# Retention of the last seven token groups: 128-token chunks on half arrays, or 64-token chunks on quarters

## The chip, the cores and the metric

The kernel is one program on one core of a Trainium2 chip. The core has a matrix engine (TensorE, PE in the profile, with its weight loads on a line of their own, PEld), a vector engine (VectorE, DVE), a scalar engine (ScalarE, ACT), a general engine (GpSimd, POOL) and a queue that issues DMA transfers (SyncE, SP). Matrix products land in PSUM, eight banks of 128 partitions by 512 floats. The metric is the device time of one launch in microseconds (us), the median over runs. Everything is computed in float32 precision or better.

## The reference

Three stages, each feeding the next: retention attention (4 batches, 8 heads, 576 tokens, 64 dimensions a head), a SoLU layer with layer norm between two weight matrices, and four ReLU experts that are summed with the weights of the tokens.

```python
# retention: q, k, v are [4, 8, 576, 64]
scores = (1 / sqrt(64)) * q @ k.T
gamma = 1 - 2 ** (-5 - arange(8))                  # one decay a head
Dmat = where(rel >= 0, gamma ** rel, 0)            # rel = query position - key position
x = (scores * Dmat) @ v                            # -> [2304 tokens, 512]
# SoLU
h = x @ w_in                                       # 512 -> 1024
solu = h * softmax(h)
ln = (solu - mean) / sqrt(var + 1e-6) * g_ln
x = ln @ w_out                                     # 1024 -> 512
# experts
p = domain_probs / sum(domain_probs)
out = sum(p[:, e] * (relu(x @ w1[e]) @ w2[e]) for e in range(4))
```

The decay lets retention be written in chunks: inside a chunk of tokens the scores are formed and masked ("qk", the DVE product "ret", and "pv"), and all that lies before the chunk enters through one 64x64 state a head ("cross"), to which each chunk adds its own keys times values ("st").

## The kernel before

The 2304 tokens are 18 groups of 128 (`NG`). Nine groups are two batches, since a batch is 4.5 groups; the fifth group of such a period (`g % 9 == 4`) therefore ends one batch in its first 64 tokens and begins the next in its last 64. The layers run in three passes of six groups (`NPASS`, `GP`). A token group of SoLU is: `h_mm` (24 products of 128x512, in two halves of 12, into a tile of the pool psA), maximum and exponential (`chain1`, `chain1e`), the softmax product with its sum (`chain2`), a squared sum on ACT (`chain2s`), the layer norm's factors on POOL (`chain3a`, `chain3m`) and its application on ACT (`chain3b`, an Identity activation on `acc`), eight transposes on PE (`tr`) whose result is split into a high and a low part by ACT (`t_hi`, two copies to `h`) and DVE (`t_lo`, two differences). After a pass's six groups `x2_mm` multiplies by w_out (24 products `b<-h,wB` a step), and the experts follow.

Retention of groups 0 to 10 is part of an order written out by hand (`ORDER`), at the start of the program. That of groups 11 to 17 (`OWN`) is not: from the first experts on, a `Recorder` collects the operations of a stretch (all of these carry line 149 in the profile, 150 in the changed kernel), gives each a due time from the costs of the PE work in program order, and lists them by a simulated schedule (`flush`): on each engine the operation with the earliest due time that is ready in the simulation goes next, on PE at most 150 operations ahead of program order, and preferably one of the group marked last (`mark`). The engines then run the lists in order; a wait at the head of a list holds all behind it. The first two groups' work (11 and 12) is recorded at the end of the experts of pass 0, the rest in pass 1's loop, between the `h_mm` halves of groups 6 to 11.

One group g of `OWN` consists of
- `att_load`, `att_v`, `att_q`: 1 MB of q, k (both layouts) and v into `tmp` (odd g) or the region `dec` (even g), and POOL's products with decays;
- `att_st`: 8 products k.T v, `sbank<-tmp 128x64` or `sbank<-dec`, which add to the state in the PSUM bank `sbank`. Two of them stand side by side on the array (column halves);
- `att_qk`: 8 products `64x128` into two banks b, two side by side on row halves;
- `att_ret`: DVE multiplies the two banks by the decay mask, 128x512 each;
- `att_state`: ACT copies the state from `sbank` into one of two buffers `states`, two copies of 64x256;
- `att_pv`: 8 products ret times v into one bank b, and 8 products state times q ("cross", `b<-tmp,st`), both on column halves, 128 columns at a time;
- `att_xh`, `att_xl`: the result's high part (ACT, 128x512) and low part (DVE).

The float32 products of retention count as two records each in the profile (x16 for 8 products). The three banks b are handed out in turn (`next_b`), also to the transposes of `tr`.

```python
for i in range(GP):                      # pass 1, groups 6 to 11
    g = g0 + i
    h_mm(g, 0)
    if own and i < 5:
        att_last(OWN[i + 1]); att_store(OWN[i + 1])
        if i + 3 < len(OWN): att_pre(OWN[i + 3])
        att_first(OWN[i + 2])
    h_mm(g, 1)
    if own and i == 4: att_last(OWN[6]); att_store(OWN[6])
```

Of the kernel before, what the change touches and what calls it, by code (L numbers as in the profile page):

```python
# [2 lines left out]

# [7 lines left out]
F32 = mybir.dt.float32  # L11
# [21 lines left out]
NJ = 9  # L33
# [59 lines left out]
class Recorder:  # L93
# [67 lines left out]
    def flush(self, done=True):  # L161
# [27 lines left out]
        waiting, order = [], []  # L189
        pe = [op for op in ops if op.engine == "PE"]  # L190
        at, idle, now = 0, 0.0, self.now
        for op in ops:
            if not left[op]:
                heapq.heappush(waiting, (ready_at[op], op.index, op))
        while len(order) < len(ops):
# [5 lines left out]
            for e in FIXED:  # L201
                if free[e] > late or not queue[e] or (e == "SP" and self.dma > late + DEPTH):
                    continue
                can = [r for r in queue[e] if not (r[2].port and self.port > late)]
                can = [r for r in can if all(busy.get(b, 0) <= late for b in r[2].banks)]
                if e == "PE":
                    while at < len(pe) and pe[at].start is not None:
                        at += 1
                    can = [r for r in can if r[2].index <= pe[at].index + AHEAD]
                    can = [r for r in can if r[2].group == self.last] or can  # L210
                if not can:
                    continue
                best = min(can)
                queue[e].remove(best)
                op = best[2]
                moved = True
                if e == "PE":
                    self.last = op.group
                    idle += now - max(free[e], begin)
                if e == "SP":  # L220
                    free[e] = now + ISSUE
                    self.dma = max(self.dma, now) + op.cost - FIXED[e]
                    op.end = self.dma + FIXED[e]
                else:
                    op.end = free[e] = now + op.cost
                if op.port:
                    self.port = op.end
                for b in op.banks:
                    busy[b] = op.end if e == "PE" else op.end + LATENCY
                op.start = now  # L230
                order.append(op)
                for s in op.after:
                    left[s] -= 1
                    ready_at[s] = max(ready_at[s], op.end + (0 if s.engine == e != "SP" else LATENCY))
                    if not left[s]:
                        heapq.heappush(waiting, (ready_at[s], s.index, s))
# [28 lines left out]
def retention_solu_moe(  # L265
# [80 lines left out]
    tmp = big.tile([P, 4608], F32, name="tmp")  # L346
    hx = big.tile([P, 3 * BLK], F32R, name="hx")
    pb = big.tile([P, 2 * BLK], F32, name="pb")
    hT = [None, None]
    area = {}  # L350

# [175 lines left out]
    def att_v(g, eng=nc.gpsimd):  # L527
        j = g % NJ
        t = grp(g)
        if j < NJ - 1:  # L530
            v, vd = (t[:, i : i + 512].rearrange("p (h t) -> p h t", h=H) for i in (1536, 2048))
            eng.tensor_tensor(
                out=vd, in0=v, in1=vtab[:, j].unsqueeze(2).to_broadcast([P, H, 64]), op=ALU.mult
            )
# [307 lines left out]
            nc.sync.dma_start(out=dst, in_=w2b[e, m].rearrange("a p t -> p a t"))  # L842

    def probs_t():
        x = pb[:, 0 : NG * E].rearrange("p (j e) -> p j e", e=E)
        y = pb[:, 128 : 128 + NG * E].rearrange("p (e j) -> p e j", e=E)
        r = pb[:, 256 : 256 + NG]
        nc.sync.dma_start(out=x, in_=probs2)
        nc.vector.tensor_reduce(out=r, in_=x, axis=AX.X, op=ALU.add)
        nc.vector.tensor_scalar_add(out=r, in0=r, scalar1=1e-9)  # L850
# [429 lines left out]
    def att_pre(g):  # L1280
        att_load(g)
        att_v(g)
        att_q(g)

    def att_first(g):
        att_st(g)
        att_qk(g)
        att_ret(g)
        att_state(g)

    def att_last(g):
        att_pv(g)
        att_xh(g)
        att_xl(g)

    def w_in_load(i):
        nc.sync.dma_start(out=wA[:, 2048 * i : 2048 * i + 2048].bitcast(F32), in_=s_in[i])
# [219 lines left out]
```

## Time and profile before

| | us |
|---|---|
| median of 3 runs (lowest, highest) | 1029.25 (1028.58, 1031.97) |
| the profiled execution | 1028.85 |
| its span in the trace | 1027.1 |
| PE busy | 1006.8 (98%) |
| DVE, ACT, POOL busy | 616.2, 526.4, 448.4 |

The chain of waits (the work that ended last, followed back) runs over PE for 93% of the span, and PE's granted clock is full in all forty slices of the page. So a stretch is read on PE: a group of PE work begins where the one before has ended unless the timeline shows an idle time in brackets. The retention that is changed lies between 382.60 us (the first st of group 11) and about 443 us; the stretch up to 389.20, before the first psA, holds no other PE work and is called the head below. The layer-norm chain and transposes of groups 8 to 11 end the stretch, and x2_mm follows.

In a timeline, the first column is the start, the second the time from the first start to the last end of the group. Ends of PE records overlap with what follows, so the time that a block takes is read from its start to the next block's start.

### The profile page before, as it was taken

What the parts mean: (1) busy time and instruction counts of PE and PEld (TensorE: products, weight loads), DVE (VectorE), ACT (ScalarE), POOL (GpSimd) and SP (SyncE); (2) the same over time, 40 slices, a digit from 0 to 9 for tenths busy, and PEclk for the clock granted to TensorE, in tenths of its full rate; (3) what the DMA queues carried; (4) which work ended last, traced back from release to release, by engine and by line L of the source; (5) the groups of instructions that cost most, each with busy time, mean ns of one, the idle gap of its engine ahead of it and who ended that gap; (6) DMA issues with size and microseconds to landing.
All of it is one profiled execution on the core that took longest, in us unless ns stands there. A gap on an engine that the chain in (4) does not pass through costs nothing.

```text
span 1027.1 us, 17077 instructions
## 1 busy us (share of the span) xinstructions
PE 1006.8 (98%) x6188; PEld 949.4 (92%) x6188; DVE 616.2 (60%) x1038; ACT 526.4 (51%) x1032; POOL 448.4 (44%) x433
## 2 busy tenths in 40 slices
PE   5999999999999999999999999999999999999998
PEld 4788998898989988899999999999899999999998
DVE  5999685586766514543736555565454736566564
ACT  3668664252534303554746556462573646555562
POOL 3443254334435012303465656564140565655554
PEclk9999999999999999999999999999999999999999
DMA  9857699899886948570847566586541748576524
GB/s 346 326 207 265 214 311 293 298 284 316 294 262 200 335 187 298 205 261 22 250 135 246 165 214 200 175 281 227 231 154 35 243 135 255 160 221 194 183 73 131
DMA packets 122788, 226.79 MB, mean 221 GB/s; under 512 B 9936, under 2 KB 57040, under 8 KB 116560
## 3 DMA queue, kind: packets, MB, share of 16 engines
q1 hardware_dynamic: 122704, 225.70, 65.9%
q8 instruction: 49, 0.80, 0.3%
q14 instruction: 35, 0.29, 0.1%
HBM read 169.00 MB, written 62.95 MB: 226 GB/s over the span
## 4 chain that ended last, share of the span: by engine, by line
PE 93%; DVE 4%; DMA 2%; ACT 1%; SPq 0%; issue 0%; ACTq 0%
PE psX L149 44%; PE b L149 29%; PE sbank L149 8%; PE psA L149 6%; DMA dec<-in_w_in 1%; DMA sx<-wA 1%; PE b L382 1%; PE b L384 1%; PE b L383 1%; PE b L604 1%; DVE wA L387 1%; PE psA L383 1%; PE psA L382 1%; PE b L610 1%; PE psA L384 0%; PE b L557 0%
## 5 line engine op out<-in xcount | busy, mean ns | idle before, releaser
L149 POOL TENSOR_TENSOR h<-tmp,h 128x384 fp32r<-128x384 f32 x128 | 129.3, 1017 | 95.0 <-ACT h L149 79.1
L149 PE MATMUL psX<-xb,wA 128*128 128x384 f32 x738 | 143.7, 334 | 0.0
L149 PEld LDWEIGHTS psX<-xb,wA 128*128 128x128 f32 x738 | 129.4, 188 | 0.3
L149 POOL TENSOR_TENSOR wA<-wA 128x512 fp32r<-128x512 f32 x74 | 97.7, 1329 | 69.6 <-ACT wA L149 69.4
L149 PE MATMUL b<-xa,wA 128*128 128x384 f32 x564 | 111.0, 334 | 0.0
L149 PEld LDWEIGHTS b<-xa,wA 128*128 128x128 f32 x564 | 99.0, 188 | 0.1
L149 ACT ACTIVATE h<-tmp 128x384 fp32r<-128x384 f32 x144 | 73.4, 521 | 30.0 <-DVE tmp L149 30.0
L149 ACT ACTIVATE tmp<-psX 128x384 f32<-128x384 f32 x122 | 59.5, 489 | 53.0 <-PE psX L149 51.1
L149 POOL TENSOR_TENSOR tmp<-tmp 128x256 f32<-128x256 f32 (+1 forms) x68 | 56.9, 853 | 57.1 <-DMA tmp<-in_w 38.3
L149 PE MATMUL psX<-wB,h 128*128 128x512 f32 x336 | 78.9, 390 | 0.0
L149 PE MATMUL psX<-xa,wA 128*128 128x384 f32 x396 | 77.4, 334 | 0.0
L149 PE MATMUL psX<-h,wA 128*128 128x384 f32 x408 | 74.9, 334 | 0.0
L149 ACT ACTIVATE tmp<-b 128x384 f32<-128x384 f32 x108 | 53.1, 492 | 42.5 <-DVE b L149 18.4
L149 PEld LDWEIGHTS psX<-wB,h 128*128 128x128 f32 x336 | 63.0, 188 | 12.8
L149 ACT ACTIVATE wA<-wA 128x512 fp32r<-128x512 f32 x74 | 46.3, 631 | 51.4 <-DMA wA<-sw 43.7
L149 PE MATMUL psA<-wA,xa 128*128 128x512 f32 x288 | 70.5, 398 | 0.8 <-DVE tmp L149 0.6
L149 PEld LDWEIGHTS psX<-h,wA 128*128 128x128 f32 x408 | 71.1, 188 | 0.0
L149 PEld LDWEIGHTS psX<-xa,wA 128*128 128x128 f32 x396 | 69.5, 188 | 0.2
L149 DVE TENSOR_TENSOR sbank<-sbank,tmp 128x384 f32<-128x384 f32 x48 | 27.2, 567 | 65.4 <-PE sbank L149 52.0
L149 PEld LDWEIGHTS psA<-wA,xa 128*128 128x128 f32 x288 | 52.7, 188 | 14.0 <-DVE tmp L149 1.0
L149 POOL TENSOR_TENSOR wC<-wC 128x512 fp32r<-128x512 f32 x38 | 50.7, 1342 | 29.0 <-ACT wC L149 28.9
L149 DVE SCALAR_TENSOR_TENSOR tmp<-b,tmp 128x384 f32<-128x384 f32 x96 | 51.5, 555 | 18.6 <-ACT tmp L149 8.4
(250 smaller groups left out, 2083.0 us busy)
## 6 DMA issues: line engine op xcount, KB each, us to landing
wA<-sw SPq DMA_DIRECT2D x298, 256.0 KB, 3.1
sw<-wA SPq DMA_DIRECT2D x32, 896.0 KB, 6.6
tmp<-in_w SPq DMA_DIRECT2D x24, 512.0 KB, 5.5
grps<-in_qkv SPq DMA_DIRECT2D x10, 1024.0 KB, 6.3
wC<-sw SPq DMA_DIRECT2D x38, 256.0 KB, 2.8
sw<-wCf SPq DMA_DIRECT2D x32, 256.0 KB, 4.1
wA<-sin SPq DMA_DIRECT2D x8, 1024.0 KB, 6.8
wB<-sout SPq DMA_DIRECT2D x8, 1024.0 KB, 8.7
```

Source lines behind the costliest of these rows:

```text
L149: op = Op(engine, lambda: call(*args, **kw), FIXED[engine] + rate * n, port)
L382: nc.tensor.matmul(ps, lh, rh, start=first, stop=False, skip_group_check=more)
L383: nc.tensor.matmul(ps, lh, rl, start=False, stop=False, skip_group_check=more)
L384: nc.tensor.matmul(ps, ll, rh, start=False, stop=last, skip_group_check=more)
L387: (eng or nc.vector).tensor_tensor(out=dst, in0=src, in1=hi.bitcast(F32), op=ALU.subtract)
L604: nc.tensor.matmul(o[r, n], v[:, 2 * n + a], ret[:, a, n], start=n == 0, stop=j == 0 and n == NP - 1)
L610: nc.tensor.matmul(o[r, n, 0:cross], st[:, n, r], qd[:, n, 0:cross], start=False, stop=n == NP - 1)
```

## The change

- Groups 11 to 17 are cut in two chunks of 64 tokens each (`sub_chunk` numbers the nine chunks of a batch). All products inside a chunk are 64x64 and stand on a quarter of the array: qk 16 products of 64 columns for two diagonal blocks of the scores (before: 8 of 128 columns, whose lower left block was needed and upper right block masked), pv 16 products, st 8 products for each chunk, of which each uses one row half.
- The state is copied out after each chunk's st (before: once a group), into a rotation of three buffers, the third in `pb`. The last chunk of a batch forms no state. Cross is done for each chunk that is not a batch's first, from that chunk's own state.
- pv and cross of a group go to two banks b, one for each chunk, 256 columns each (before: one bank). The copies `xh` and `xl` are two of 128x256 each, ret four of 64x256; the memset for group 13 is dropped.
- The scheduler's choice on PE may take from each marked group only the first operation in program order that is not yet listed (`heads`). This rule holds for all recorded work, the transposes and x2_mm too.
- `att_v` runs for group 17 too, the first memset on POOL covers the third buffer, and `probs_t` uses a place in `pb` behind it.

```diff
--- before.py
+++ after.py
@@ -1,4 +1,5 @@
 import heapq
+from collections import deque
 from contextlib import ExitStack
 
 import numpy as np
@@ -189,6 +190,9 @@
         waiting, order = [], []
         pe = [op for op in ops if op.engine == "PE"]
         at, idle, now = 0, 0.0, self.now
+        heads = {}
+        for op in pe:
+            heads.setdefault(op.group, deque()).append(op)
         for op in ops:
             if not left[op]:
                 heapq.heappush(waiting, (ready_at[op], op.index, op))
@@ -207,6 +211,7 @@
                     while at < len(pe) and pe[at].start is not None:
                         at += 1
                     can = [r for r in can if r[2].index <= pe[at].index + AHEAD]
+                    can = [r for r in can if r[2] is heads[r[2].group][0]]
                     can = [r for r in can if r[2].group == self.last] or can
                 if not can:
                     continue
@@ -216,6 +221,7 @@
                 moved = True
                 if e == "PE":
                     self.last = op.group
+                    heads[op.group].popleft()
                     idle += now - max(free[e], begin)
                 if e == "SP":
                     free[e] = now + ISSUE
@@ -346,6 +352,7 @@
     tmp = big.tile([P, 4608], F32, name="tmp")
     hx = big.tile([P, 3 * BLK], F32R, name="hx")
     pb = big.tile([P, 2 * BLK], F32, name="pb")
+    states.append(pb[:, 0:512].rearrange("p (n t) -> p n t", n=NP))
     hT = [None, None]
     area = {}
 
@@ -527,7 +534,7 @@
     def att_v(g, eng=nc.gpsimd):
         j = g % NJ
         t = grp(g)
-        if j < NJ - 1:
+        if j < NJ - 1 or g >= EARLY:
             v, vd = (t[:, i : i + 512].rearrange("p (h t) -> p h t", h=H) for i in (1536, 2048))
             eng.tensor_tensor(
                 out=vd, in0=v, in1=vtab[:, j].unsqueeze(2).to_broadcast([P, H, 64]), op=ALU.mult
@@ -842,9 +849,9 @@
             nc.sync.dma_start(out=dst, in_=w2b[e, m].rearrange("a p t -> p a t"))
 
     def probs_t():
-        x = pb[:, 0 : NG * E].rearrange("p (j e) -> p j e", e=E)
-        y = pb[:, 128 : 128 + NG * E].rearrange("p (e j) -> p e j", e=E)
-        r = pb[:, 256 : 256 + NG]
+        x = pb[:, 512 : 512 + NG * E].rearrange("p (j e) -> p j e", e=E)
+        y = pb[:, 600 : 600 + NG * E].rearrange("p (e j) -> p e j", e=E)
+        r = pb[:, 700 : 700 + NG]
         nc.sync.dma_start(out=x, in_=probs2)
         nc.vector.tensor_reduce(out=r, in_=x, axis=AX.X, op=ALU.add)
         nc.vector.tensor_scalar_add(out=r, in0=r, scalar1=1e-9)
@@ -1282,16 +1289,74 @@
         att_v(g)
         att_q(g)
 
+    HALVES = [slice(0, 64), slice(64, 128)]
+
+    def sub_chunk(g, s):
+        return (2 * (g % NJ) + s) % NJ
+
+    def short_state(g, s):
+        return states[(2 * g + s - 2 * EARLY + 1) % 3]
+
+    def short_st(g, s):
+        nc.mark()
+        t = grp(g)
+        kn, vd = (t[:, i : i + 512].rearrange("p (h t) -> p h t", h=H) for i in (1024, 2048))
+        q = sub_chunk(g, s)
+        if q == NJ - 1:
+            return
+        for h in range(H):
+            n, a = divmod(h, 2)
+            nc.tensor.matmul(
+                st_ps[HALVES[a], n], kn[HALVES[s], h], vd[HALVES[s], h], start=q == 0 and n == 0,
+                stop=n == NP - 1, skip_group_check=q > 0,
+            )
+        for r in HALVES:
+            copy(short_state(g, s + 1)[r, :, r], st_ps[r])
+
     def att_first(g):
-        att_st(g)
-        att_qk(g)
-        att_ret(g)
-        att_state(g)
+        short_st(g, 0)
+        nc.mark()
+        t = grp(g)
+        qt, kt = (t[:, i : i + 512].rearrange("p (n t) -> p n t", n=NP) for i in (0, 512))
+        qk = [next_b()[:, 0:256].rearrange("p (n t) -> p n t", n=NP) for a in range(2)]
+        for n in range(NP):
+            for c in HALVES:
+                for a, r in enumerate(HALVES):
+                    nc.tensor.matmul(qk[a][c, n], kt[r, n, c], qt[r, n, c], start=True, stop=True)
+        ret = (area["dec"], tmp)[g % 2][:, 3072:3584].rearrange("p (a n t) -> p a n t", a=2, n=NP)
+        for a in range(2):
+            for c in HALVES:
+                nc.vector.tensor_tensor(out=ret[c, a], in0=qk[a][c], in1=dmask[c, a, :, c], op=ALU.mult)
+        att[g] = ret
+        short_st(g, 1)
 
     def att_last(g):
-        att_pv(g)
-        att_xh(g)
-        att_xl(g)
+        nc.mark()
+        t = grp(g)
+        v = t[:, 1536:2048].rearrange("p (h t) -> p h t", h=H)
+        qd = t[:, 2560:3072].rearrange("p (n t) -> p n t", n=NP)
+        ret = att.pop(g)
+        o = [next_b()[:, 0:256].rearrange("p (n t) -> p n t", n=NP) for _ in range(2)]
+        alone = [sub_chunk(g, s) == 0 for s in range(2)]
+        for n in range(NP):
+            for s, c in enumerate(HALVES):
+                for a, r in enumerate(HALVES):
+                    nc.tensor.matmul(
+                        o[s][r, n], v[c, 2 * n + a], ret[c, a, n], start=n == 0, stop=alone[s] and n == NP - 1
+                    )
+        for s, c in enumerate(HALVES):
+            if not alone[s]:
+                for n in range(NP):
+                    for r in HALVES:
+                        nc.tensor.matmul(
+                            o[s][r, n], short_state(g, s)[:, n, r], qd[:, n, c], start=False, stop=n == NP - 1
+                        )
+        hi, lo = (att_to(g)[:, i].rearrange("p (n s t) -> s p n t", n=NP, s=2) for i in range(2))
+        for s in range(2):
+            nc.scalar.activation(out=hi[s], in_=o[s], func=AF.Copy, scale=F64_SCALE)
+            nc.vector.scalar_tensor_tensor(
+                out=lo[s], in0=o[s], scalar=F64_SCALE, in1=hi[s].bitcast(F32), op0=ALU.mult, op1=ALU.subtract
+            )
 
     def w_in_load(i):
         nc.sync.dma_start(out=wA[:, 2048 * i : 2048 * i + 2048].bitcast(F32), in_=s_in[i])
```

Recorded order on PE, the head, before: `sbank` is the state's bank, `tmp` holds group 11 and `dec` group 12, b1 is pv's bank, b2 and b0 are qk's.

```order
L149 MATMUL sbank_69<-dec_3018 64x64 x8
L149 MATMUL b1_67<-tmp_88 64x128 x4
L149 MATMUL b2_68<-dec_3018 128x128 x2
L149 MATMUL b0_66<-dec_3018 128x128 x2
L149 MATMUL b1_67<-tmp_88 64x128 x3
L149 MATMUL b1_67<-tmp_88,st1_83 64x128
L149 MATMUL b1_67<-tmp_88 64x128
L149 MATMUL b1_67<-tmp_88,st1_83 64x128 x7
L149 MATMUL psA1_1_3244<-wA_84,xa_86 128x512 x12
```

The same place after, from group 11's second st to the first psA (of qk for group 12, b0 and b1 by turns, two of fifteen rows are shown).

```order
L150 MATMUL sbank_69<-tmp_88 64x64 x8
L150 MATMUL b1_67<-tmp_88 64x64
L150 MATMUL sbank_69<-dec_3019 64x64 x8
L150 MATMUL b1_67<-tmp_88 64x64
L150 MATMUL b2_68<-tmp_88 64x64 x2
L150 MATMUL b1_67<-tmp_88,st1_83 64x64 x8
L150 MATMUL b2_68<-tmp_88,pb_90 64x64 x8
L150 MATMUL b0_66<-dec_3019 64x64
L150 MATMUL sbank_69<-dec_3019 64x64 x8
L150 MATMUL b1_67<-dec_3019 64x64
L150 MATMUL b0_66<-dec_3019 64x64
L150 MATMUL psA1_1_3303<-wA_84,xa_86 128x512 x12
```

There are now four blocks on `sbank` before the first psA instead of two, and between the second and the third stands only a single pv product.

PE at the end of the stretch, before: the last psA (`h_mm` of group 11), then the transposes `b<-tabs,acc` of groups 9 and 10 and the steps of x2_mm, `b<-h1,wB`.

```order
L149 MATMUL psA1_0_3243<-wA_84,xa_86 128x512 x12
L149 MATMUL b2_68<-tabs_75,acc_87 128x128 x4
L149 MATMUL b0_66<-tabs_75,acc_87 128x128 x4
L149 MATMUL b1_67<-h1_554,wB_85 128x384 x24
L149 MATMUL b2_68<-tabs_75,acc_87 128x128 x4
L149 MATMUL sbank_69<-tabs_75,acc_87 128x128 x4
L149 MATMUL b0_66<-h1_554,wB_85 128x384 x24
```

The same place after; the rows of `tmp` are the ends of cross of group 17.

```order
L150 MATMUL psA1_0_3302<-wA_84,xa_86 128x512 x12
L150 MATMUL b2_68<-tmp_88,st1_83 64x64 x8
L150 MATMUL b0_66<-tmp_88,pb_90 64x64 x8
L150 MATMUL b1_67<-tabs_75,acc_87 128x128 x4
L150 MATMUL b2_68<-tabs_75,acc_87 128x128 x4
L150 MATMUL b0_66<-tabs_75,acc_87 128x128 x4
L150 MATMUL b1_67<-tabs_75,acc_87 128x128 x4
L150 MATMUL b2_68<-tabs_75,acc_87 128x128 x4
L150 MATMUL sbank_69<-tabs_75,acc_87 128x128 x4
L150 MATMUL b0_66<-h1_555,wB_85 128x384 x24
L150 MATMUL b1_67<-h1_555,wB_85 128x384 x24
```

The last psA has moved ahead of pv, cross and the transposes of group 8, and the transposes of group 10 (the rows on b2 and sbank) ahead of the first step of x2_mm.

ACT's list there, after: the two `wA<-b` are xh of group 17, `h1<-b` are t_hi of group 8, `acc<-psA` is the exponential of group 11, `h2<-b` are t_hi of group 9, and `acc<-acc` is the Identity of group 10 that its transposes read.

```order
L150 ACTIVATE wA_84<-b2_68 128x4x64
L150 ACTIVATE wA_84<-b0_66 128x4x64
L150 ACTIVATE h1_555<-b1_67 128x4x128
L150 ACTIVATE h1_555<-b2_68 128x4x128
L150 ACTIVATE acc_87,stats_80<-psA1_0_3302,stats_80 128x1024
L150 ACTIVATE h2_984<-b0_66 128x4x128
L150 ACTIVATE h2_984<-b1_67 128x4x128
L150 ACTIVATE acc_87<-acc_87,stats_80 128x1024
```

Before, ACT's list held xh of group 17 and t_hi of group 8 ahead of the last psA's exponential too, but these came while PE was still at that psA.

## Rows read from the trace of the kernel before

**Rows 1.** The page: span, PE's busy time, the chain by engine.
```profile
span 1027.1 us, 17077 instructions
PE 1006.8 (98%) x6188; PEld 949.4 (92%) x6188; DVE 616.2 (60%) x1038; ACT 526.4 (51%) x1032; POOL 448.4 (44%) x433
PE 93%; DVE 4%; DMA 2%; ACT 1%; SPq 0%; issue 0%; ACTq 0%
```

**Rows 2.** Windows: stretch, busy time of each engine, granted clock, DMA share.
```profile
382.60:389.20 6.60, 6.49 (x97) 5.70 (x96) 3.33 (x5) 1.07 (x3) 0.00 (x0) 1.00 0.11 42
389.20:446.76 57.56, 57.56 (x506) 46.52 (x506) 29.30 (x49) 27.30 (x47) 15.41 (x24) 1.00 0.66 243
```

**Rows 3.** Timeline of PE: one group with narrow cross, the next whole.
```profile
402.75 0.69 PE L149 MATMUL b<-tmp,st 128*64 128x64 f32 x16
403.37 3.03 PE L149 MATMUL psA<-wA,xa 128*128 128x512 f32 x12
406.33 0.73 PE L149 MATMUL sbank<-dec 128*64 128x64 f32 x16
406.99 1.16 PE L149 MATMUL b<-dec 64*128 64x128 f32 x16
408.08 3.06 PE L149 MATMUL psA<-wA,xa 128*128 128x512 f32 x12
411.07 1.15 PE L149 MATMUL b<-dec 128*64 128x128 f32 x16
411.99 1.09 PE L149 MATMUL b<-dec,st 128*64 128x128 f32 x16
413.02 3.02 PE L149 MATMUL psA<-wA,xa 128*128 128x512 f32 x12
```

**Rows 4.** Timeline of PE: the head, in which group 11's pv starts alone.
```profile
382.60 0.73 PE L149 MATMUL sbank<-tmp 128*64 128x64 f32 x16
383.26 1.16 PE L149 MATMUL b<-tmp 64*128 64x128 f32 x16
384.35 0.73 PE L149 MATMUL sbank<-dec 128*64 128x64 f32 x16
385.20 1.09 PE L149 MATMUL b<-tmp 128*64 128x128 f32 x8
386.21 1.17 PE L149 MATMUL b<-dec 64*128 64x128 f32 x16
387.31 0.54 PE L149 MATMUL b<-tmp 128*64 128x128 f32 x3
...
389.20 3.06 PE L149 MATMUL psA<-wA,xa 128*128 128x512 f32 x12
```

**Rows 5.** Timeline of ACT and of DVE: state copies and ret in the head.
```profile
383.37 0.78 ACT L149 ACTIVATE st<-sbank 64x256 f32<-64x256 f32 x2 [31.49 <-PE sbank L149]
384.45 1.29 DVE L149 TENSOR_TENSOR tmp<-b,tabs 128x512 f32<-128x512 f32 x2 [0.99 <-PE b L149]
```

**Rows 6.** Timeline of PE: the end of the stretch.
```profile
443.07 1.09 PE L149 MATMUL b<-tabs,acc 128*128 128x128 f32 x8
443.92 3.00 PE L149 MATMUL psA<-wA,xa 128*128 128x512 f32 x12
446.76 1.03 PE L149 MATMUL b<-tabs,acc 128*128 128x128 f32 x8
447.55 4.43 PE L149 MATMUL b<-h,wB 128*128 128x384 f32 x24
451.88 0.63 PE L149 MATMUL b<-tabs,acc 128*128 128x128 f32 x4
```

**Rows 7.** Timeline of ACT: the end of the stretch.
```profile
443.17 0.60 ACT L149 ACTIVATE wA<-b 128x512 fp32r<-128x512 f32 x1 [0.53 <-PE b L149]
443.76 1.09 ACT L149 ACTIVATE h<-b 128x512 fp32r<-128x512 f32 x2
448.22 1.12 ACT L149 ACTIVATE acc<-psA,stats 128x1024 f32<-128x1024 f32 x1 [3.37 <-DVE stats L149]
449.32 1.08 ACT L149 ACTIVATE h<-b 128x512 fp32r<-128x512 f32 x2
450.28 1.25 ACT L149 ACTIVATE acc<-acc,stats 128x1024 f32<-128x1024 f32 x1
```

**Rows 8.** Timeline of DVE: the low parts of a transposed group.
```profile
444.41 1.28 DVE L149 TENSOR_TENSOR h<-b,h 128x512 fp32r<-128x512 f32 x2
```

**Rows 9.** Groups of PE instructions by form: the transposes, with idle time before them.
```profile
L149 PE MATMUL b<-tabs,acc 128*128 128x128 f32 x88 | 11.9, 274 | 0.5 <-DVE h L149 0.5
```

## Prediction

> **What bounds the kernel now.** I read the page first: PE is busy for 1006.8 of a span of 1027.1 us, and the chain that ended last runs over PE for 93% [rows 1]. Then the windows of the stretch that is changed. From the first psA at 389.20 to the end of the last at 446.76 PE is busy in all of its 57.56 us, at the full granted clock, while DVE has 29.30 and ACT 27.30 us of work; in the head before it PE is busy for 6.49 of 6.60 us, and ACT has only 1.07 us of work [rows 2]. So a microsecond more or less on PE here is a microsecond of the kernel, and work that is added to ACT, DVE or POOL is free until PE has to wait for it. The timelines say what a block of PE work takes and what stands between an engine's result and PE's next block [rows 3 to 8].
>
> **What a block costs.** I take start-to-start times. Cross on 128 columns takes 413.02 - 411.99 = 1.03 us, on 64 columns 403.37 - 402.75 = 0.62, both with a change of the array's tile shape behind them; so 64 columns fewer are worth 0.41. pv, with none behind it (cross has its shape), takes 411.99 - 411.07 = 0.92. A change of shape hence costs 1.03 - 0.92 = 0.11; by the st block (0.66 against 0.92 - 0.41 = 0.51) it is 0.15, by qk (1.09 against 0.92) 0.17 [rows 3]; by psA with and without one, 2.99 against 2.84 [rows 3, 6], 0.15. I take 0.14. A wide block is 0.92, a narrow one 0.51, and in each two tiles work side by side with eight records each.
>
> After the change all blocks are narrow. A qk or pv block has 32 records of 64 columns on four quarters, so eight a quarter: 0.51 if all four work side by side. No row shows four; if only two do, it is 16 steps, 1.02 at most (twice 0.51) and 0.92 at least (as many columns as a wide block has). I take 0.51, because the four quarters differ in rows and columns just as the pairs do that already run side by side, and keep both ends. st and cross of a chunk have 16 records on two tiles: 0.51.
>
> **The sum of blocks behind the head.** Before: 4 st, 1 narrow cross, and 16 wide blocks (5 qk, 6 pv, 5 cross): 5 x 0.51 + 16 x 0.92 = 17.3 us. After: 8 st, 5 qk, 6 pv, 11 cross, that is 30 x 0.51 = 15.3. That is 2.0 less, though products are more: the wide blocks' gain is half eaten by the doubled st and cross. Changes of shape, counted in the recorded order from the first psA to the last transposes: 26 before, 35 after, since pv and cross no longer share a shape and since single products of qk or pv have been pulled ahead of a psA four times. 9 x 0.14 = +1.3. Net -0.7.
>
> **The head.** Before, it takes 6.60 us, of which 385.20 to 386.21 is half of pv alone on one column half [rows 4]. Without waits the new one would be 9 narrow blocks (4 st, 2 qk, 1 pv, 2 cross) and 4 changes, 5.2 us, 1.4 less. But four st blocks now share the one bank `sbank`, and each waits until ACT has copied the last state out. Copies start 0.77 after an st block starts and take 0.78 for the pair [rows 4, 5]; PE goes on about 0.10 after a result (the first ret product ends at 384.45 + 0.65, pv starts at 385.20). So st follows st by 1.65 at the earliest: 382.60, 384.25, 385.90. Between the first two PE has qk, 0.51; between the second and third a single pv product. Then pv and the first chunk's cross to 386.41 + 2 x 0.51 + 0.14 = 387.57; in ACT's list the first xh stands between the two copies of the third state, so copies end at about 388.45 and the fourth st starts at 388.55, followed by the rest of qk: first psA at 388.55 + 0.51 + 0.51 + 0.14 = 389.7, against 389.20: **+0.5**. The ends are -1.4 (waits all covered) and +1.0 (quarters two at a time).
>
> **The middle.** A second st stands behind a psA in all groups from 14 to 16, so its wait (1.65 from st to st) is covered by 2.99 us of psA [rows 3]. One place is not covered: qk of group 17 needs the bank b0 of the transposes of group 7, whose second half now stands behind a psA, with pv, cross and st between, some 2.6 us of PE work, while the bank is released by a copy to h and a difference (0.54 and 0.64, half of [rows 7, 8]), possibly behind an Identity of 1.25. That is 0 to 0.7; I take **+0.4**.
>
> **The end of the stretch.** Before, the last psA ends at 446.76, and the Identity of group 10 ends at 450.28 + 1.25 = 451.53, that is 4.0 us after the transposes of group 9 have ended (447.55). PE doesn't notice: it has a step of x2_mm there, 4.33 us, and starts group 10's transposes at 451.88 [rows 6, 7]. After the change these transposes stand ahead of x2_mm, and PE's list is strict in order as far as waits go. Counting from the end of the last psA: pv and two cross blocks with two changes 1.8, transposes of groups 8 and 9, 0.85 and 0.79, then group 10 would start at 3.45. ACT meanwhile has to do, in its order: xh of chunk 2 after cross has ended, to 2.3; t_hi of group 8 from 2.45, 1.09, to 3.54; the exponential of group 11 with its read, 1.10 from start to start, to 4.64; t_hi of group 9, 1.09, to 5.73 (its second half waits for b1, which t_lo of group 8 has left by 3.7); Identity, 1.25, to 6.98. PE starts group 10's transposes at 7.08 instead of 3.45: **+3.6**. x2_mm, which could have run, is queued behind. Before, the exponential found ACT idle for 3.37 us [rows 7]: xh and t_hi of group 8 had been done during the psA. That cover is gone because the last psA has moved ahead of them. The ends: 0, if ACT were early by as much, and 3.9. Nothing is late next: x2_mm's first step started without a wait at 447.55, 0.8 us after the last psA, and would start 7 us later behind it.
>
> **The rest.** The rule `heads` also reorders the transposes beside x2_mm of pass 2. In the trace all 88 transposes together waited for 0.5 us [rows 9]; I take +0.3, between 0 and 0.7 (as large a wait again as at the bank above). Twelve further state copies of 0.39 on ACT, seven more pieces each of xh and of xl, one more product on POOL for group 17: hidden by ACT's and DVE's 30 us and POOL's 42 us without work in the stretch [rows 2], but for the waits above; without that cover the copies alone would cost 12 x 0.39 = 4.7. The larger memset lies before PE's first work, behind the first loads. The load of group 13 is issued after cross of group 11 as before, and qk's first product waits for it one psA earlier; I take 0, at most one psA of 2.99 were it late.
>
> **Sum.** 0.5 - 0.7 + 0.4 + 3.6 + 0.3 = +4.1. The profiled execution took 1028.85 us, 0.4 less than the median of 1029.25, so 1028.85 + 4.1 = 1033.0.
>
> **Rivals.**
> A. The forecast, 1033.0; its own range is 1030.5 to 1035.5.
> B. Quarters don't work four at a time. Then 11 blocks behind the head cost 0.41 to 0.51 more each, 4.5 to 5.6, and the head about 0.4 (its qk lies beside the state copies): 1033.0 + 5.4, about 1038.4. For it: no row shows more than two tiles at once, and in the st block 16 records in 0.51 us are one every 32 ns. Against it: nothing in the pairs shows a limit of records rather than of columns.
> The Trainium skill ("TensorE: Matmul & The Clock Gate", section "Wait — 56ns, not 53.3ns?") says that one matmul starts at least about 25 ns after another however small it is. By that rule the 32 records of a qk or pv block would take 0.80 us, an estimate, and 13 such blocks would make the time about 1036. The st block's 32 ns neither contradicts it nor bears it out, and I count it with B.
> C. No change: st uses one row half only, so qk's records on the other half may run beside it, as cross of another chain ran beside pv's second half in the head (three pv records from 387.31, then cross in between). Where st and qk now adjoin without a wait, about 9 times, half a block of 0.26 to 0.31 is saved: -2.6, so 1030.4.
> D. Faster: the end stall doesn't arise. Its place is the wait of group 10's transposes for the Identity; its price is 3.6; it decides if ACT reaches the Identity before PE has ended group 9's transposes. Then 1029.4 is left, and with C's overlap, which needs the same free-running PE, 1026.8; with the head's waits covered as well (-1.9) 1025. Against it: before, even with its work done ahead, ACT ended the Identity 4.77 after the last psA [rows 6, 7], and PE now has 3.45 us of work to there.
>
> **Chances.** A 0.52, B 0.20, C 0.18, D 0.10. A change under 0.3%, 3.1 us, can't be told from none here. Of A about a third lies within that bound (below 1032.3), of C nearly all, of D four tenths: within 0.36. Slower: two thirds of A and B, 0.55. Faster: 0.09. The range is 1027.0 to 1038.8: below it lies most of D, above it half of B's upper part, together under 0.2.
>
> **What would show it.** Right: three waits of PE on ACT before `sbank` blocks in the head and a first psA about 0.5 us later; qk blocks of 32 records in 0.5 to 0.7 us; one PE idle of 3 to 4 us before the third pair of transposes, put down to ACT. Wrong: qk blocks near 1 us (B); st records among qk's (C); transposes of group 10 without a wait (D); or the larger loss in a stretch that has no retention in it, which no term here has.

## The result and the profile after

The changed kernel takes 1036.35 us, the median of 9 runs (1030.81 to 1038.68), against 1029.25 before (9 runs, 1028.58 to 1031.97); the ratio is 1.0058, 95% interval 1.0038 to 1.0078, so some 6 us slower (the two medians differ by 7.1). Run again on another chip (below) it was 1.0041 [1.0025, 1.0057]. The profiled execution of it took 1034.64 us. The forecast of 1033.0 had the side and the mechanism; what it lacked is in TensorE's clock and in a gain of the list rule `heads`.

The page of the kernel after: span, busy time, chain by engine, to be laid beside [rows 1].

```profile
span 1032.8 us, 17958 instructions
PE 1006.7 (97%) x6604; PEld 948.9 (92%) x6604; DVE 618.9 (60%) x1058; ACT 530.6 (51%) x1051; POOL 444.4 (43%) x435
PE 90%; DVE 5%; DMA 2%; ACT 1%; issue 1%; POOL 0%; SPq 0%; ACTq 0%; DVEq 0%
```

PE has 416 more instructions and the same busy time, while the span is 5.7 us longer: PE is idle for longer, and in part it is busy at half its clock. To see where, I measured four stretches from the starts of the same blocks in every trace (us):

| kernel | first st starts at | head, to the first psA | middle and end, to group 11's transposes | from there to the end |
|---|---|---|---|---|
| before | 382.60 | 6.60 | 76.07 | 561.8 |
| after | 383.43 | 8.34 | 79.03 | 562.0 |
| after, run again (e5) | 383.81 | 7.08 | 79.52 | 562.0 |

The start of the first st varies from 382.60 to 387.47 over the traces, whatever the kernel, so I leave it out of all that follows. In nine of the thirteen traces, of both kinds of kernel, the granted clock is half for some 3 us or twice that near 20 us or between 46 and 53 (in after it is 0.72 from 20 to 26), long before the retention that was changed; the three latest starts (e1, e4, e9) are those of the traces whose only early fall begins near 49.

Windows of the kernel after, head and middle, with columns as in [rows 2]:

```profile
383.43:391.77 8.34, 6.87 (x193) 6.20 (x193) 3.11 (x7) 2.93 (x9) 0.00 (x0) 0.80 0.35 111
391.77:445.14 53.37, 53.37 (x761) 42.61 (x760) 29.34 (x63) 28.59 (x56) 16.35 (x25) 1.00 0.64 240
```

From the first psA to the end of the last one, PE is still busy in all of its time and at the full clock. The losses lie on either side: in the head, where 1.47 us are idle and the clock was 0.80, and behind the last psA.

Timeline of PE after: one whole group of the middle, to be laid beside [rows 3].

```profile
399.62 0.69 PE L150 MATMUL b<-tmp 64*64 64x64 f32 x30
400.13 0.64 PE L150 MATMUL sbank<-tmp 64*64 64x64 f32 x16
400.70 3.02 PE L150 MATMUL psA<-wA,xa 128*128 128x512 f32 x12
403.65 0.69 PE L150 MATMUL b<-tmp 64*64 64x64 f32 x32
404.28 0.69 PE L150 MATMUL b<-tmp,pb 128*64 128x64 f32 x16
404.89 3.04 PE L150 MATMUL psA<-wA,xa 128*128 128x512 f32 x12
```

From start to start, qk takes 0.51 us, st 0.57, pv 0.63 and cross 0.61, the last three with a change of shape behind them. (Two of this qk's 32 records stand ahead of the psA before it, from 396.42, and take 0.25 there.) The four quarters do work side by side: 30 records in 0.51 us, one every 17 ns, as many columns a quarter as a tile of a pair had in [rows 3]. By the rule of the Trainium skill that the prediction cited ("TensorE: Matmul & The Clock Gate", section "Wait — 56ns, not 53.3ns?"), 32 records would take at least about 0.80 us, an estimate; this case's trace contradicts it for records on four tiles: pv has 32 in 0.63, the change of shape included.

Timeline of PE after, the head: compare [rows 4]. In brackets is PE's idle time before the row, and what ended it.

```profile
383.43 0.62 PE L150 MATMUL sbank<-tmp 64*64 64x64 f32 x13
...
384.99 0.51 PE L150 MATMUL sbank<-tmp 64*64 64x64 f32 x10 [0.41 <-ACT pb L150]
...
386.54 1.01 PE L150 MATMUL sbank<-dec 64*64 64x64 f32 x14 [0.87 <-ACT st L150]
...
388.44 1.12 PE L150 MATMUL b<-tmp,st 128*64 128x64 f32 x16
389.35 0.90 PE L150 MATMUL b<-tmp,pb 128*64 128x64 f32 x16
...
390.69 0.62 PE L150 MATMUL sbank<-dec 64*64 64x64 f32 x14 [0.19 <-ACT st L150]
```

Three of the four st blocks wait for ACT's copy of the state before, as forecast. ACT's timeline there, beside [rows 5]:

```profile
384.15 0.78 ACT L150 ACTIVATE pb<-sbank 64x256 f32<-64x256 f32 x2 [31.45 <-PE sbank L150]
385.72 0.77 ACT L150 ACTIVATE st<-sbank 64x256 f32<-64x256 f32 x2 [0.78 <-PE sbank L150]
```

Copies start 1.57 apart (1.65 forecast). But the first cross block takes 388.44 to 389.35, 0.91 where in the middle it takes 0.51 to 0.61. That is the clock. Windows of the kernel after in the head and behind the last psA; the granted clock is the third column from the end:

```profile
386.00:387.00 1.00, 0.46 (x8) 0.47 (x10) 0.18 (x1) 0.47 (x2) 0.00 (x0) 0.75 0.00 0
387.00:389.00 2.00, 2.00 (x54) 1.88 (x52) 0.00 (x0) 0.00 (x0) 0.00 (x0) 0.50 0.03 8
452.00:454.00 2.00, 2.00 (x10) 2.00 (x11) 0.97 (x3) 1.66 (x4) 0.80 (x3) 0.50 1.02 361
455.00:460.00 5.00, 5.00 (x31) 5.00 (x30) 0.74 (x2) 1.46 (x3) 0.00 (x0) 1.00 1.05 397
```

Twice in these stretches the granted clock is half for a few us, 1.2 of 2.4 GHz, each time with or right behind PE's waits. In the kernel before it is 1.00 in the head and from 446.76 to 456.00.

Timeline of PE after, behind the last psA, beside [rows 6]:

```profile
445.07 0.69 PE L150 MATMUL b<-tmp 64*64 64x64 f32 x32
...
446.77 1.67 PE L150 MATMUL b<-tabs,acc 128*128 128x128 f32 x12
448.84 0.66 PE L150 MATMUL b<-tabs,acc 128*128 128x128 f32 x4 [0.40 <-DVE h L150]
451.86 1.12 PE L150 MATMUL b<-tabs,acc 128*128 128x128 f32 x4 [2.36 <-ACT acc L150]
452.76 1.06 PE L150 MATMUL sbank<-tabs,acc 128*128 128x128 f32 x4
```

And ACT there, beside [rows 7]:

```profile
446.42 0.85 ACT L150 ACTIVATE wA<-b 128x256 fp32r<-128x256 f32 x2 [4.74 <-PE b L150]
447.47 1.14 ACT L150 ACTIVATE h<-b 128x512 fp32r<-128x512 f32 x2 [0.19 <-PE b L150]
448.50 1.11 ACT L150 ACTIVATE acc<-psA,stats 128x1024 f32<-128x1024 f32 x1
449.59 1.08 ACT L150 ACTIVATE h<-b 128x512 fp32r<-128x512 f32 x2
450.55 1.26 ACT L150 ACTIVATE acc<-acc,stats 128x1024 f32<-128x1024 f32 x1
```

This is the chain the prediction wrote down, piece by piece: xh, t_hi of group 8, exponential, t_hi of group 9, Identity, and group 10's transposes at its end, 6.79 us behind the last psA (7.08 forecast). PE has nothing for 2.36 us, while x2_mm's first step stands behind. The transposes' group of the page's kind, beside [rows 9], has its idle time up from 0.5 to 3.3:

```profile
L150 PE MATMUL b<-tabs,acc 128*128 128x128 f32 x88 | 12.8, 284 | 3.3 <-ACT acc L150 2.4 <-DVE h L150 0.9
```

### The profile page after: what moved, and what is told of

The parts are those of the page before. It is cut to its first block, busy times and chain, and to the rows that moved or that the text cites. A ratio compares the mean times of both kernels' runs of the same rounds, so it can differ in the third digit from the quotient of the medians.

```text
span 1032.8 us, 17958 instructions
## 1 busy us (share of the span) xinstructions
PE 1006.7 (97%) x6604; PEld 948.9 (92%) x6604; DVE 618.9 (60%) x1058; ACT 530.6 (51%) x1051; POOL 444.4 (43%) x435
## 4 chain that ended last, share of the span: by engine, by line
PE 90%; DVE 5%; DMA 2%; ACT 1%; issue 1%; POOL 0%; SPq 0%; ACTq 0%; DVEq 0%
PE psX L150 43%; PE b L150 28%; PE sbank L150 8%; PE psA L150 6%; DMA sx<-wA 1%; DMA tabs<-in_tab 1%; DVE wA L394 1%; PE b L611 1%; PE b L389 1%; PE b L391 1%; PE b L390 1%; PE b L564 1%; PE psA L390 1%; PE psA L389 1%; DVE wCf L150 1%
```

## The experiments

Each time is a median over one job's runs, and each ratio is to the kernel before on the same chip. "Stretch" is head, middle and end together in the profile (before 82.67, after 87.37 and, run again, 86.60). The edits are shown in short: lines that only carry an edit through are left out.

**e1, the list rule alone**, added to the kernel before, and once more as e10.

```diff
+ heads.setdefault(op.group, []).append(op)
+ can = [r for r in can if r[2] is heads[r[2].group][0]]
+ heads[op.group].pop(0)
```

> The kernel before with nothing but the rule that PE's products of a marked group are listed in program order (heads). In its recorded order x2_mm's first step still stands between the transposes of groups 9 and 10. Theory 1 (the loss comes from the narrow chunks' places in the order, not from this rule): 1029.3 +- 1.0 us, no idle of PE over 0.5 us between 383 and 470 us, granted clock as before (0.999). Theory 2 (the rule itself costs, by stopping products that could run early): 1031 or more.

1029.63 (1027.53 to 1032.56), ratio 0.9982 [0.9967, 0.9996]. The rule costs nothing; it gains a little, and it doesn't put group 10's transposes ahead of x2_mm. The stretch is 81.51, 1.16 shorter: 0.47 in the head (6.13) and 0.67 behind it (75.40). Rows of PE in the same kernel run again (e10), head and middle:

```profile
385.68 0.43 PE L149 MATMUL b<-tmp 128*64 128x128 f32 x2 [0.16 <-DVE tmp L149]
386.04 1.39 PE L149 MATMUL b<-dec 64*128 64x128 f32 x16
387.36 0.98 PE L149 MATMUL b<-tmp 128*64 128x128 f32 x13
...
411.76 1.04 PE L149 MATMUL b<-dec,st 128*64 128x128 f32 x16
```

In the head two of pv's records stand alone ahead of qk, where before eight did [rows 4]: 0.36 for 1.01, with 1.32 for 1.10 in the qk behind them. The rest of pv and cross takes 1.89 in both, by turns before, one after the other here. In the middle cross takes 0.97 (psA starts at 412.73) for 1.03 before and st 0.61 for 0.66: the change of shape behind them costs less.

**e2, x2_mm's first step first**: the kernel after, with group 10's transposes recorded as part of the same marked piece, behind x2_mm's first step.

```diff
+ if m == 0 and p == 1: tr(g0 + GP - 2, False)   # behind x2_mm(0, 0)
- if m in (1, 2):
+ if m == 2 or (m == 1 and p > 1):
```

> The changed kernel with the transposes of group 10 listed behind the first step of x2_mm; all else as in the changed kernel. Theory 1 (the end stall is an order's doing, and the half clock behind it follows from PE's idle time): the idle of 2.4 us and the half clock from 451.5 to 454.5 go, some 3.5 us less than the changed kernel; the half clock in the head stays. Theory 2 (the clock falls for another reason): only the idle goes, 2.4 us less, and x2_mm's first products still take twice as long.

1031.95, ratio 1.0006 [0.9993, 1.0019]. PE's timeline in e2, behind cross of group 17:

```profile
450.27 0.66 PE L150 MATMUL b<-tabs,acc 128*128 128x128 f32 x4 [0.40 <-DVE h L150]
450.68 4.41 PE L150 MATMUL sbank<-h,wB 128*128 128x384 f32 x24
454.93 4.32 PE L150 MATMUL b<-h,wB 128*128 128x384 f32 x24
```

x2_mm starts without a wait, so its inputs were there; only the order kept it back. Middle and end fall from 79.03 to 75.11: the order of this one piece costs 3.9, half clock included.

**e3, the second half of each state copy of groups 11 and 12 on DVE**, and **e4, both edits**.

```diff
+ if i and g < EARLY + 2: nc.vector.tensor_copy(out=short_state(g, s + 1)[r, :, r], in_=st_ps[r])
+ else: copy(short_state(g, s + 1)[r, :, r], st_ps[r])
```

> The changed kernel with the second of the two state copies of groups 11 and 12 on DVE, so that ACT and DVE copy side by side; in the recorded order group 11's pv and cross now stand between its second st and group 12's first. Theory 1: the head (first st to first psA) falls from 8.3 us to about 6.2, of which 1.1 is the half clock that no longer comes, and the end stall stays. Theory 2 (half clock is the narrow products' doing, not the waits'): waits shrink by about 1 us, pv and cross still take 1.0 and 0.9 us instead of 0.5 each, head about 7.3.

> Both edits at once: state copies of groups 11 and 12 on ACT and DVE, and x2_mm's first step ahead of the transposes of group 10. Theory 1 (two waits and the half clock behind each are the whole loss): the changed kernel's middle, 1.7 us shorter than before, remains, so 1026.5 to 1028.5, granted clock 0.999, and a spread over runs of 3 us or less as in the kernel before. Theory 2 (half clock or spread come from the narrow products): clock 0.995 or lower in part of the runs, 1029 to 1034.

e3: 1033.97, 1.0034 [1.0020, 1.0048], with a head of 7.11; e4: 1031.42, 1.0011 [0.9998, 1.0023], head 8.57. Neither the head of 6.2 nor the 1026.5 to 1028.5 of the expectations came. Two rows of e3's DVE say why the head isn't shorter than e5's 7.08:

```profile
383.94 0.43 DVE L150 COPY pb<-sbank 64x256 f32<-64x256 f32 x1 [0.28 <-ACT pb L150]
384.40 1.55 DVE L150 TENSOR_TENSOR tmp<-b,tabs 64x256 f32<-64x256 f32 x4
```

ret now starts behind the copy, and pv waits for ret: one wait replaced another. And e4 runs the same list in the head as e3 but takes 1.46 us longer, with waits of 0.47 ahead of its second and its fourth st; its granted clock there:

```profile
390.00:394.00 4.00, 3.98 (x82) 3.61 (x85) 1.23 (x4) 0.77 (x2) 0.00 (x0) 0.57 0.38 78
```

In e3's head it was 1.00. So the fall belongs to the execution, not to the list, and costs about 1.5.

**e5, the kernel after unchanged**, and **e6, its waits filled**: three products of 256 columns between group 11's qk and its second st, six behind that st, twenty ahead of group 10's transposes. They write banks that are overwritten before they are read, and the scheduler is told that they cost next to nothing.

```diff
+ def fill(ps): nc.tensor.matmul(ps, neg[:, 0], neg.rearrange("p i t -> p (i t)"), start=True, stop=True); nc.ops[-1].cost = 1e-4
+ for _ in range(3 if (g, s) == (11, 1) else 0): fill(pool["a"][1][:, 0:256])   # before the st block
+ for _ in range(6 if (g, s) == (11, 1) else 0): fill(pool["a"][1][:, 0:256])   # behind it
+ for _ in range(20 if g == 10 else 0): fill(tps[g][1].rearrange("p n t -> p (n t)")[:, 0:256])
```

> The changed kernel unaltered, beside the next three on one chip. Theory 1: from the head's first st on it is again 4 to 6 us longer than the kernel before, with waits of 0.4 and 0.9 us in the head and 2.4 us at the end, and half clock behind at least one of them.

> The changed kernel with products into unused PSUM in the waits: 3 of 128x256 ahead of group 11's second st, 6 behind it, 20 ahead of group 10's transposes (some 0.11 us each; they compute nothing that is used). The order of all else is kept. Theory 1 (PE's idle time lets the granted clock fall): the waits stay or are filled, the clock stays at full, head about 7.2 to 7.6 instead of 8.3, x2_mm's first products at full speed, 1.5 to 2 us less than the changed kernel. Theory 2 (the narrow products by themselves, or something off PE, let it fall): half clock as before in the head, no gain.

e5: 1035.76 (1033.0 to 1037.85), 1.0041 [1.0025, 1.0057]; the mean granted clock over its runs is 0.9949, over those of before 0.9974. Its profile has a head at the full clock, and then a fall at the end:

```profile
383.81:390.89 7.08, 5.39 (x193) 4.78 (x192) 3.11 (x7) 2.93 (x9) 0.00 (x0) 1.00 0.36 106
452.00:454.00 2.00, 2.00 (x9) 2.00 (x8) 1.18 (x2) 1.77 (x5) 1.01 (x3) 0.50 0.97 347
```

e6: 1033.26, 1.0027 [1.0012, 1.0042], at a mean clock of 0.9976. By the medians it is 2.5 us faster than e5 in the same job, by the means 1.9, by the ratios 1.4, and the two ratios' intervals overlap. Its PE at the end:

```profile
447.75 2.63 PE L150 MATMUL sbank<-neg 128*128 128x256 f32 x20
450.36 0.66 PE L150 MATMUL b<-tabs,acc 128*128 128x128 f32 x4
450.85 0.60 PE L150 MATMUL sbank<-tabs,acc 128*128 128x128 f32 x4
```

The windows of the same stretch:

```profile
450.00:452.00 2.00, 2.00 (x17) 1.82 (x16) 1.16 (x3) 2.00 (x5) 0.40 (x2) 1.00 0.97 338
452.00:455.00 3.00, 3.00 (x19) 3.00 (x19) 1.24 (x2) 1.65 (x2) 0.60 (x2) 1.00 1.02 371
```

Group 10's transposes come as late as ever: ACT's Identity ends at 450.30 (449.04 + 1.26), and they start at 450.36. Yet with PE kept at work the clock stays at 1.00, the transposes take 0.84 from start to x2_mm instead of 1.62 in after (451.86 to 453.48) and 1.23 in e5, and 1.7 us of the middle and end are gone against e5 (77.78 for 79.52). Its head takes 7.17, like e5's, where the clock held too. So part of the loss at the end was not the idle time but the clock behind it.

**e7, two st blocks of the head moved**: e2, with pv of group 11, the preparation of group 13 and group 12's first half behind the first psA.

```diff
+ if own and i == 0: att_last(OWN[0]); att_pre(OWN[2]); att_first(OWN[1]); h_mm(g, 1)   # in pass 1
- att_last(OWN[0]); att_pre(OWN[2]); att_first(OWN[1])   # at the experts' tail
- h_mm(g, 1)
+ if not own or i > 0: h_mm(g, 1)
```

> e2 (x2_mm's first step ahead of group 10's transposes) with group 11's pv and cross and all of group 12 recorded behind the first half of h_mm, so that psA products stand between the four st blocks. Theory 1: no wait over 0.5 us between the first st and x2_mm, no half clock there; from the first st to the transposes of group 11 about 79.5 us (before 82.7, the kernel with heads alone 81.5), total 1026 to 1028. Theory 2 (quarters cost something that waits and clock don't show): no faster than the kernel with heads alone.

1030.44, 0.9997 [0.9982, 1.0013]. The head has one wait of 0.41 left, but the same work now needs a bank sooner, and the fall comes there:

```profile
409.81 0.91 PE L150 MATMUL b<-dec 64*64 64x64 f32 x27 [1.43 <-DVE wA L150]
```

The window behind it:

```profile
410.00:414.00 4.00, 4.00 (x53) 3.42 (x49) 1.60 (x5) 2.00 (x3) 1.18 (x2) 0.57 0.96 373
```

Its stretch is 83.66, longer than before and not the 79.5 expected. (The bank wait that the prediction feared before group 17 was real in kind, at another place and in another order.)

**e8, a wait given to the kernel before**: group 11's state is copied three times; the scheduler counts the further copies as nothing.

```diff
+ for k in range(3 if g == 11 else 1):
      for a in range(2):
          copy(states[(g + 1) % 2][r, :, r], st_ps[r])
          if k: nc.ops[-1].cost = -LATENCY
```

> The kernel before with group 11's state copied three times, so that group 12's st must wait about 1.6 us in the head, among wide blocks; nothing else moved. Theory 1 (waits let the clock fall, whatever the blocks): 1.5 to 2 us longer by the wait, and half clock of about 3 us behind it, with pv and cross at twice their time, in part or all of the runs: 1031 to 1033. Theory 2 (narrow products are needed for it): only the wait, granted clock 1.00 throughout the head.

1032.68, 1.0010 [0.9992, 1.0028]; mean clock 0.9977, as before's. PE at the wait:

```profile
385.85 0.73 PE L149 MATMUL sbank<-dec 128*64 128x64 f32 x16 [1.39 <-ACT st L149]
```

The window behind it:

```profile
386.00:392.00 6.00, 6.00 (x71) 5.26 (x70) 1.98 (x3) 1.36 (x3) 0.00 (x0) 1.00 0.26 59
```

One wait of 1.39 among wide blocks made the head 1.09 longer and no fall. So not every wait of this size brings one.

**e9, the order of the end given to the wide kernel**: e1 with group 10's transposes recorded ahead of x2_mm, in one marked piece with its first three steps.

```diff
+ if m == 0 and p == 1: tr(g0 + GP - 2)   # ahead of x2_mm(0, 0)
+ x2_mm(0, m, m > 2 or p > 1)   # a mark of its own only then
- if m in (1, 2):
+ if m == 2 or (m == 1 and p > 1):
```

> e1 (the kernel before with the rule heads) with nothing changed but that group 10's transposes are listed ahead of x2_mm's first step; retention in wide blocks. Theory 1 (the end stall belongs to this order, not to narrow chunks): PE idles about 4.0 us there (in the kernel before the Identity ended 4.0 us after group 9's transposes), half clock of some 3 us behind it costs 1 to 1.5 more, together 5 us over e1: 1034 to 1036. Theory 2 (the stall needs the chunks' extra ACT work): idle under 1.5 us, at most 2 us over e1.

> e1 again with more rounds, as the fastest kernel so far. Theory: from the first st on 1.0 to 1.2 us less than before, all of it in the head and in pv and cross that no longer take turns; ratio 0.998 to 0.9995.

e9: 1036.07, 1.0045 [1.0028, 1.0062]; e10 in the same job: 1028.74, 0.9977 [0.9965, 0.9989]. PE in e9:

```profile
454.45 1.94 PE L149 MATMUL b<-tabs,acc 128*128 128x128 f32 x8 [4.68 <-DVE h L149]
456.04 4.24 PE L149 MATMUL b<-h,wB 128*128 128x384 f32 x16
```

The windows there:

```profile
449.00:453.00 4.00, 0.77 (x8) 0.53 (x5) 2.66 (x4) 2.81 (x5) 0.00 (x0) 0.86 1.02 305
453.00:456.00 3.00, 1.55 (x8) 1.58 (x9) 1.30 (x4) 2.05 (x4) 1.01 (x3) 0.50 1.07 404
456.00:459.00 3.00, 3.00 (x12) 3.00 (x11) 1.38 (x2) 1.89 (x3) 0.00 (x0) 0.55 1.03 378
```

Without one product on a quarter, this order costs 7.3 us against e10. In the profiles middle and end differ by 6.74 (82.14 and 75.40): 4.68 are idle, and 1.8 lie in the transposes and x2_mm behind, at half clock in part. The quarters aren't needed for the loss at the end; the place of one piece in PE's list makes it.

**e11, e7 with the scheduler told the price of a quarter**: its cost of a 64x64 product halved.

```diff
+ parts = [tuple(aps[k].ap)[0][1] for k in ("in0", "out")]
+ if parts == [64, 64]: rate /= 2
```

> e7 with a truer cost of a 64x64 product in the scheduler (half of what it assumed; the blocks measured 0.5 us, it reckoned with 1.07). In the recorded order no single products are pulled ahead any more, and st of group 14 is not listed behind a bank that is still read. Theory 1 (what is left of e7's loss is the 1.4 us wait at group 14 and the half clock behind it): no wait over 0.5 us, no half clock, 642.5 to 643.5 us from the first st to the end of the span (before 644.5, e1 643.3), ratio 0.998. Theory 2 (the order has another late input): a wait of 1 us or more in another place.

1030.46, 0.9991 [0.9980, 1.0001]; the bank wait is 0.69 instead of 1.43 (none over 0.5 was expected), the clock is 1.00 from 383 to 500 and the stretch is 81.64. That is 1.0 below before and no better than e10's 81.53, which has no quarters at all: 1028.74 in the same job. e10, the kernel before with the list rule alone, has the lowest median of all and beats both kernels.

## Why the prediction came out as it did

**Blocks and changes of shape** (-0.7 forecast, +0.4 for the bank): right in kind. Narrow blocks take 0.51 to 0.52 where no change of shape stands behind them, so B (quarters two at a time) is refuted. C's overlap is there for a few records of qk among st's last ones (from 408.26 in after), but st and qk take 1.08 together (407.86 to 408.94), so nothing is saved by it. The bank wait before group 17 didn't come, as the window from 391.77 with PE busy throughout shows. With the order at the end mended (e2) middle and end are 75.11, 0.96 less than before, a wait of 0.40 before group 9's transposes included; forecast was -0.3. But the list rule with wide chunks (e1, e10) is 0.67 less there too, so that the quarters' own part is 0.29, as forecast with that wait in place of the bank's. A change of shape is 0.11 to 0.12 behind pv and 0.05 to 0.10 behind cross and st, less than the 0.14 I took from [rows 3]; in e10 it is less than before as well, with wide blocks. That this makes up all of the difference is not shown. The prediction gave the list rule no part in the middle, and +0.3 in the rest.

**The head** (+0.5): right where the clock held. e5's head is 7.08, +0.48, with waits of 0.41, 0.87 and 0.41. In after's own profile it was +1.74, since the clock fell: 28 of pv's records take 1.03, and the cross blocks 0.91 and 0.82. What was missing is in the sum that ends "first psA at 388.55 + 0.51 + 0.51 + 0.14 = 389.7": it prices the blocks behind a wait at 0.51 like all others, and not as blocks that can run at half clock. Before's head also had 0.47 in it that the list rule takes away without quarters (e1), so that against e1 e5's head is +0.95.

**The end** (+3.6): its size is right by e2, which gains 3.9. The working had the chain on ACT to within 0.3 us (6.79 against 7.08), and D is refuted. But the idle time is 2.76 (0.40 and 2.36), not 3.6: PE ran dry at 449.50, 4.43 behind the last psA, and not at 3.45. The remaining 1.2 is clock: the transposes of group 10 take 1.62 instead of 0.82 to the next piece, and x2_mm from there to group 11's transposes 17.32, against 16.90 before. (e2 keeps the wait of 0.40; 2.36 and 1.2 are 3.6 of its 3.9.) So the sum of the term was right by luck, made of a stall too large and a clock that wasn't thought of.

**The rest** (+0.3): from group 11's transposes to the end, +0.2. It doesn't belong to the rule `heads`: e1 and e10 have 561.8, as before has. A wait of 0.25 on ACT's `h` stands behind group 11's transposes in after and e5, and in all traces with group 10's transposes ahead of x2_mm (e3, e6 and e9 too), and in no other: it goes with the order at the end.

**The sum.** From e5's profile: 0.48 + 3.45 + 0.2 = +4.1, as forecast; from after's: 1.74 + 2.96 + 0.2 = +4.9. That e5 meets the forecast is luck in part: it holds 1.2 or more of half clock, and the gain of the list rule that wide chunks have as well (1.16 in e1), and the prediction had neither. By the ratios the loss is 6.0 [3.9, 8.0] and 4.2 [2.6, 5.9]. The upper part comes with the clock: after's fastest run, 1030.81, has a granted clock of 1.00, its slowest, 1038.68, 0.993. How often a run has one fall, two or none was not counted from traces, only from the mean clocks (0.9949 against 0.9974), in which the falls before 53 us count too. The time of about 1036 that stands below rival B should read about 1037 by its own working (13 blocks, 0.29 more each); nothing hangs on it.

**Where the expected gain went.** Quarters and list rule together make the stretch 1.0 shorter once order, waits and cost are mended (e11). The list rule alone makes it 1.1 shorter, with wide blocks (e10). So of the quarters' own gain nothing is left. The waits of 0.41, 0.69 and 0.40 that e11 still has are enough to explain it: without them, and without e10's 0.16, e11's stretch would be some 1.2 shorter than e10's (an estimate: 81.64 - 1.50 against 81.53 - 0.16). No run shows quarters without these waits.

Why the scheduler set group 10's transposes first stays open. Its table prices the 64x64 products as if two at most ran at once, so that a block counts 1.07 where the chip takes 0.51, but that isn't the reason: the list that e11's cost alone gives for the kernel after still has them first, and so has the list without the rule `heads` (lists only, neither was run). With wide chunks the rule leaves x2_mm first (e1).

## What to carry over

In a list that an engine works through in strict order, ask of each piece that moved ahead of a large independent one what it waits for: here 0.8 us of transposes in front of 8.4 us of ready products (e2's first two steps of x2_mm) cost 3.9. Price a wait of PE by its idle time and then by the blocks behind it at half clock, 1.2 to 1.5 us here, as a chance and not a certainty; where the wait can't be removed, products that nobody reads gave back 1.7 us in e6's profile (1.4 to 2.5 over its runs, not sure by them alone). And test a change's helper rule by itself: here it gained 1.16 in the stretch, where the change lost.

## What the runs showed of the hardware that was not expected

- The granted clock fell to half behind waits that add up to 1.3 us among narrow blocks (after's head: 0.41 and 0.87), with or behind 0.40 and 2.36, behind one of 0.47 with pv held up by ret after it (e4), one of 1.43 (e7) and in one of 4.68 (e9), but not behind one of 1.39 among wide blocks (e8), and not in every execution of one list (e3 and e4, after and e5). Each of these falls lasted some 3 us, e9's about twice that. Whether narrow products before a wait make it likelier stays open.
- Four tiles of 64x64 take 30 fp32 records of 64 columns in 0.51 us, and records of a block with a free tile start ahead of the end of the block before: qk records stand between st's last ones (384.21 in e5: one record of qk, then st again).
